# Seven half-block products instead of eight in the last layer's first product, on 512-token blocks

## The chip, the cores and the metric

One core of one Trainium2 chip. The metric is the device time of one execution in microseconds (us). Five engines work side by side, each through its own queue of instructions: TensorE (PE; its weight loads are shown apart, as PEld), VectorE (DVE), ScalarE (ACT), GpSimd (POOL), and SyncE (SP), which issues all the DMAs. Matrix products go to PSUM, eight banks of 128 partitions x 512 floats; everything else lies in SBUF or in DRAM.

## What is computed

Attention with a cumulative bias (4 batches, 8 heads, 576 tokens, 64 per head), then two feed-forward layers, the second with a low-rank mixing of the tokens ahead of it:

```python
def _moe_ref(x, g_ln, w_ch1, w_ch2):            # layer 0; x: (4, 576, 512)
    xn = (x - mu) / np.sqrt(var + 1e-06) * g_ln
    ch = np.maximum(xn @ w_ch1, 0.0) @ w_ch2    # 512 -> 2048 -> 512
    return x + ch

def _moe2_ref(x, U, V, w_ch1, w_ch2):           # layer 1; U: (576, 32), V: (32, 576)
    h = x.transpose(0, 2, 1) @ U @ V
    u = x + h.transpose(0, 2, 1)
    ch = np.maximum(u @ w_ch1, 0.0) @ w_ch2     # 512 -> 2048 -> 512
    return u + ch
```

Weights come as 64-bit floats and are turned into 32-bit ones on the chip.

## The kernel before

**Precision.** Products of the layers run on numbers in two parts: a value is split into hi (fp32r) and lo (the rest), and a product is three matmuls, hi.hi, lo.hi and hi.lo. So each 128 x 128 tile of weights is streamed against by three matmuls, and each of the three has its own weight load.

**Blocks and steps.** The 576 tokens of a batch are block A (256) and block B (320). The hidden 2048 are 16 tiles of 128 (`m`). One step (`st`) is a block and a tile: `mlp1` (lines 1026 to 1066) takes the 4 k-tiles of the 512 inputs, 12 matmuls of 256 or 320 columns (lines 1058 to 1060), into one PSUM bank; ScalarE's relu makes `hh` and a VectorE operation `hl` (lines 1064, 1065). `mlp2` (lines 1068 to 1111) runs `LAG` = 2 steps later: 12 matmuls (lines 1092 to 1094) add the tile's share to the 512 outputs, which stay in PSUM banks (`acc`, and `ps` for block B) until a run of steps of one block ends; then line 1102 adds them to `x`, and in layer 1 line 1106 writes `out`. `GROUPS` (line 31) lists the order of the blocks: layer 0 in six groups, layer 1 as A and B of one batch after the other, each group once with one half of the tiles and once with the other. Attention for later blocks runs between the steps of layer 0.

**Layer 1's input.** `t_items` (line 944) multiplies each finished layer 0 block by U and stores x and that product in DRAM (`x_dr`, `t_dr`). `u_load` and `u_items` (lines 991 to 1020) fetch them, multiply by V (line 1013), add into `x` (line 1017) and split it into `xh` and `xl` (lines 355 to 367), for a block a few steps ahead; `xh` and `xl` have two buffers each, so that the next block's can be made beside the current.

**Weights.** `w_ahead` (line 535) converts and splits a half tile (512 KB in DRAM) during layer 0 and stores it to `w_dr`; `w_split` (line 515) loads the halves from there into 16 SBUF buffers `w`, eight tiles' worth. `mix_prep_v` (line 932) prepares V into two `pB` buffers.

**Order.** Nothing is placed by hand on the engines: each piece is recorded as an operation with a priority (its step), a duration estimate and a choice of engines, and class `Plan` (line 86) lists them in the order in which a greedy walk through the estimates would start them, in five passes. A buffer tag has a fixed number of buffers (`sb` lines 321 to 326), and except for `ps` they are taken in program order. Two operations that go by SBUF alone on VectorE and GpSimd are planned one after the other (`port`).

## Time and profile before

| | us |
|---|---|
| median of 3 runs | 1088.88 (1086.11 to 1090.93) |
| the profiled execution | 1090.13 |
| its span, first to last instruction | 1088.4 |
| TensorE busy in the span | 1066.7 (98%) |
| VectorE busy | 605.4 (56%) |
| ScalarE busy | 497.7 (46%) |
| GpSimd busy | 135.8 (12%) |
| DMA, mean rate | 213.24 MB, 196 GB/s |

A row of a group of instructions reads: line of the kernel, engine, operation, output <- inputs with their shapes, count | busy time, mean ns of one | idle time of the engine ahead of them and what ended it. Matmuls overlap in time and their ends are modelled, so a matmul's own cost is read from the distance between two starts. A DMA row gives the count, the size and the median time from issue to landing.

### The profile page before, as it was taken

The page shows a single profiled execution, that of the slowest core. Times are in us where ns is not written, and L with a number is a line of the kernel's source. Part 1 is how long each engine was busy: PE and PEld are TensorE (multiplying, and loading weights), DVE is VectorE, ACT ScalarE, POOL GpSimd, SP SyncE. Part 2 cuts the span into 40 slices and gives each one's busy share as a digit, 9 for nine tenths or more (in the row PEclk, how much of TensorE's full clock was granted, in tenths as well). Part 3 has the DMA queues.
Part 4 walks back from the last instruction along what each step waited for, and adds up shares of the span by engine and source line. Part 5 has one row for each costly group of instructions (what it writes and reads, how often), then busy time and mean ns, then how long its engine had stood idle before and what let it go on. Part 6 is the DMA issues. An engine that isn't in the chain of part 4 may idle for free.

```text
span 1088.4 us, 20805 instructions
## 1 busy us (share of the span) xinstructions
PE 1066.7 (98%) x7969; PEld 1021.6 (94%) x7969; DVE 605.4 (56%) x1457; ACT 497.7 (46%) x1201; POOL 135.8 (12%) x301
## 2 busy tenths in 40 slices
PE   8998999999999999999999999999999999999998
PEld 6687999999999989988999999999999999999998
DVE  8998976876887766847864535632312331233121
ACT  7988865765765656736654323521211211111110
POOL 1113222231321212301110000000000000000000
PEclk9998999999999999999999999999999999999999
DMA  7998993129735693492368599881154116211710
GB/s 240 352 331 309 357 344 112 60 70 335 250 123 171 223 340 129 149 347 99 131 203 299 190 387 373 296 347 50 49 169 141 49 49 219 91 50 52 258 60 34
DMA packets 76483, 213.24 MB, mean 196 GB/s; under 512 B 11456, under 2 KB 23744, under 8 KB 76384
## 3 DMA queue, kind: packets, MB, share of 16 engines
q1 hardware_dynamic: 76384, 211.91, 55.9%
q8 instruction: 63, 1.03, 0.4%
q14 instruction: 36, 0.29, 0.1%
HBM read 166.71 MB, written 54.60 MB: 203 GB/s over the span
## 4 chain that ended last, share of the span: by engine, by line
PE 84%; DMA 5%; ACT 5%; DVE 4%; issue 1%; POOL 0%; SPq 0%; ACTq 0%; POOLq 0%; DVEq 0%
PE ps L1058 12%; PE ps L1059 11%; PE ps L1060 11%; PE acc L1092 8%; PE acc L1094 8%; PE acc L1093 8%; PE ps L793 4%; PE ps L746 3%; PE ps L1092 3%; PE ps L1093 3%; PE ps L1094 3%; PE ps L697 2%; ACT t L707 1%; PE ps L693 1%; PE ps L675 1%; DMA w<-w_dr 1%
## 5 line engine op out<-in xcount | busy, mean ns | idle before, releaser
L1058 PE MATMUL ps<-xh,w 128*128 128x256 f32 (+1 forms) x1024 | 313.3, 306 | 3.5 <-DVE mx L680 2.6
L1060 PE MATMUL ps<-xl,w 128*128 128x256 f32 (+1 forms) x1024 | 304.0, 297 | 1.0 <-POOL xl L362 1.0
L1059 PE MATMUL ps<-xh,w 128*128 128x256 f32 (+1 forms) x1024 | 303.9, 297 | 0.0
L1065 DVE SCALAR_TENSOR_TENSOR hl<-ps,hh 128x256 fp32r<-128x256 f32 (+1 forms) x256 | 116.5, 456 | 318.2 <-ACT hh L1064 317.1
L1064 ACT ACTIVATE hh<-ps 128x256 fp32r<-128x256 f32 (+1 forms) x256 | 104.2, 408 | 381.6 <-PE ps L1060 380.3
L1092 PE MATMUL acc<-hh,w 128*128 128x256 f32 (+1 forms) x768 | 229.6, 299 | 1.0 <-ACT hh L1064 1.0
L1094 PE MATMUL acc<-hl,w 128*128 128x256 f32 (+1 forms) x768 | 223.9, 292 | 0.5 <-DVE hl L1065 0.5
L1093 PE MATMUL acc<-hh,w 128*128 128x256 f32 (+1 forms) x768 | 223.7, 291 | 0.0
L1058 PEld LDWEIGHTS ps<-xh,w 128*128 128x128 f32 x1024 | 195.4, 191 | 8.5 <-DVE mx L680 2.9
L1060 PEld LDWEIGHTS ps<-xl,w 128*128 128x128 f32 x1024 | 195.0, 190 | 1.3 <-POOL xl L362 1.3
L1059 PEld LDWEIGHTS ps<-xh,w 128*128 128x128 f32 x1024 | 195.6, 191 | 0.5
L1092 PEld LDWEIGHTS acc<-hh,w 128*128 128x128 f32 x768 | 146.0, 190 | 4.3 <-issue 2.0
L1094 PEld LDWEIGHTS acc<-hl,w 128*128 128x128 f32 x768 | 145.9, 190 | 0.8 <-DVE hl L1065 0.7
L1093 PEld LDWEIGHTS acc<-hh,w 128*128 128x128 f32 x768 | 146.1, 190 | 0.5
L707 ACT ACTIVATE t<-t,mx 128x128 f32<-128x128 f32 (+4 forms) x144 | 83.1, 579 | 32.8 <-DVE mx L701 26.5
L1094 PE MATMUL ps<-hl,w 128*128 128x320 f32 x256 | 79.1, 309 | 0.0
L1093 PE MATMUL ps<-hh,w 128*128 128x320 f32 x256 | 79.1, 309 | 0.0
L1092 PE MATMUL ps<-hh,w 128*128 128x320 f32 x256 | 79.1, 309 | 0.0
L360 DVE TENSOR_TENSOR pB<-ps,pB 128x512 fp32r<-128x512 f32 (+2 forms) x114 | 63.4, 570 | 19.2 <-ACT pB L355 18.6
L355 ACT ACTIVATE pB<-ps 128x512 fp32r<-128x512 f32 (+4 forms) x121 | 59.7, 503 | 25.5 <-PE ps L746 23.0
L746 PE MATMUL ps<-ident,t 128*128 128x128 f32 x400 | 64.5, 277 | 6.2 <-POOL t L723 2.0
L701 DVE CUSTOM_DVE_ANT_0 t<-ps,causal 128x128 f32<-128x128 f32 (+3 forms) x128 | 56.9, 487 | 10.6 <-PE ps L697 10.0
(130 smaller groups left out, 1459.7 us busy)
## 6 DMA issues: line engine op xcount, KB each, us to landing
w<-w_dr SPq DMA_DIRECT2D x176, 512.0 KB, 7.1
w_dr<-wr SPq DMA_DIRECT2D x48, 512.0 KB, 4.5
wr<-w1a SPq DMA_DIRECT2D x16, 512.0 KB, 5.9
wr<-w2a SPq DMA_DIRECT2D x16, 512.0 KB, 6.1
w_dr<-w SPq DMA_DIRECT2D x16, 512.0 KB, 6.2
wr<-w1b SPq DMA_DIRECT2D x16, 512.0 KB, 5.0
wr<-w2b SPq DMA_DIRECT2D x16, 512.0 KB, 7.1
qkvB<-qkv_b SPq DMA_DIRECT2D x32, 224.0 KB, 5.4
```

Of the source, the lines that this page charges most:

```text
L355: "act": ((51 if psum else 94) + 0.8333 * n, lambda: nc.scalar.activation(out(), a(), AF.Copy)),
L360: alts = {"dve": (68 + 1.042 * n, lambda: nc.vector.tensor_tensor(out=out(), in0=a(), in1=b(), op=op))}
L707: act(prio, K, lambda t=t, mx=mx, o=o, K=K, x=x, y=nt * z + x: nc.scalar.activation(t[:, o:o + K], t[:, o:o + K], AF.Exp, bias=mx[:, (1 if ...
L746: nc.tensor.transpose(ps[:, 128 * j:128 * (j + 1)], t[:, c:c + 128], ident.tile)
L1058: nc.tensor.matmul(ps[:, :n], w[:, 0, sl], xh[:, k, :n], start=k == 0, stop=False)
L1059: nc.tensor.matmul(ps[:, :n], w[:, 1, sl], xh[:, k, :n], start=False, stop=False)
L1060: nc.tensor.matmul(ps[:, :n], w[:, 0, sl], xl[:, k, :n], start=False, stop=k == KT - 1)
L1064: act(st - 1000, n, lambda: nc.scalar.activation(hh[:, :n], ps[:, :n], AF.Relu), [ps], [hh], 51)
L1065: dve(st - 1000, n, lambda: nc.vector.scalar_tensor_tensor(out=hl[:, :n], in0=ps[:, :n], scalar=0.0, in1=f(hh[:, :n]), op0=ALU.max, op1=AL ...
L1092: nc.tensor.matmul(a, w[:, 0, sl], hh[:, :n], start=new, stop=False)
L1093: nc.tensor.matmul(a, w[:, 1, sl], hh[:, :n], start=False, stop=False)
L1094: nc.tensor.matmul(a, w[:, 0, sl], hl[:, :n], start=False, stop=last and (z == 1 or blk == "B"))
```

## The change

Layer 0 stays as it is. In layer 1:

- The blocks are now C, the first 512 tokens of a batch, and T, the last 64 tokens of all four batches as one block of 256: `LAST = ("C0", "C1", "C2", "C3", "T0")`. Each block goes through all 16 tiles once, in alternating directions.
- **First product of C.** Two tiles (a pair) form a 2 x 2 scheme: two halves of the tokens (256 each), two halves of the 512 inputs (two k-tiles each), two tiles. Eight half-block products give the result directly; here seven do, on sums and differences of operands (Strassen's scheme in Winograd's form). `c_operands` makes the seven operands on the side of the tokens, each split into hi and lo, in the buffers xc, v, xh, xh, xl, xl and t, t: one buffer set for all batches. `w1_ahead` makes the weight sums during layer 0 and stores seven units (hi and lo) per pair; `w1_load` fetches them, 1.84 MB per pair, into two sets of `qk` and `pB` buffers. `mlp1c` runs the products, 6 matmuls of 256 columns each; seven VectorE additions and a copy per pair put the results together in `hh` and `hl` buffers, from which relu and split make the hidden values, in four buffers borrowed from `w`.
- **Second product of C** (`mlp2c`): 12 matmuls per tile as before, each 512 columns wide, into four PSUM banks. Twelve of the 16 tiles of `w2` stay loaded (`W2SLOTS`).
- **T** goes through `mlp1` and `mlp2` as an A block would, on the plain units of the stored weights; x, xh and xl lie in `wr` buffers. Its loads and its `out` DMAs move pieces of 64 tokens (256 bytes).
- V's two parts move from `pB` to `t`; the preparation of layer 1's weights is spread over steps 16 to 132 (`W1`) where it ran over steps 40 to 142, beside other small moves.

```diff
+LAST = ("C0", "C1", "C2", "C3", "T0")
+W2SLOTS = 12
-W1 = (67, 128)
+W1 = (16, 66, 50)
...
+    P.borrow("hw", "w", 2 * WSLOTS - W2SLOTS)
...
+    def w1_ahead(p, gate):
...
+        (ta, tb), s, h = ts, P.buf("wr", [128, 1024]), P.buf("wr", [128, 1024], F32R)
...
+        copy(prio, 256, lambda: s[:, 768:], lambda: tb[:, :256], [tb], [(s, 3)], psum=True)
+        sub(0, lambda: tb[:, 256:], lambda: s[:, 768:], ALU.add, [tb, (s, 3)])
+        sub(2, lambda: ta[:, :256], lambda: s[:, 768:], ALU.subtract, [ta, (s, 3)])
+        sub(1, lambda: s[:, :256], lambda: ta[:, :256], ALU.subtract, [ta, (s, 0)])
+        sub(3, lambda: ta[:, 256:], lambda: s[:, 256:512], ALU.subtract, [ta, (s, 1)])
...
+    OPERANDS = {1: "xc", 5: "v", 6: "xh", 7: "xl", 2: "t", 4: "xh", 3: "xl"}
...
+        known(1, quarter(x0, 0), key(x0, 0))
+        diff(5, quarter(x0, 1), quarter(x0, 0), key(x0, 1), key(x0, 0))
+        diff(6, quarter(x1, 1), sums(5), key(x1, 1), [tmp[5]])
+        known(6, sums(6), [tmp[6]])
+        known(5, sums(5), [tmp[5]])
+        diff(7, quarter(x1, 1), quarter(x0, 1), key(x1, 1), key(x0, 1))
+        known(7, sums(7), [tmp[7]])
+        known(2, quarter(x1, 0), key(x1, 0))
+        diff(4, quarter(x1, 0), sums(6), key(x1, 0), [tmp[6]])
+        known(4, sums(4), [tmp[4]])
+        known(3, quarter(x1, 1), key(x1, 1))
...
+    ORDER = {(0, 0): (1, 6), (0, 1): (7, 5), (1, 0): (2, 4), (1, 1): (3,)}
...
+    def mlp1c(st, half):
...
+                for k in range(2):
+                    sl = slice(128 * k, 128 * (k + 1))
+                    nc.tensor.matmul(region(r), w[:, u, 0, sl], part(r, 0)[:, k], start=new and k == 0, stop=False)
+                    nc.tensor.matmul(region(r), w[:, u, 1, sl], part(r, 0)[:, k], start=False, stop=False)
+                    nc.tensor.matmul(region(r), w[:, u, 0, sl], part(r, 1)[:, k], start=False, stop=k == 1 and (r == 3 or not new))
...
+        if (m % 2, half) == (0, 0):
+            s[1] = P.buf("hh", [128, 256])
+            copy(st - 1000, 256, lambda d=s[1]: d.tile, lambda: region(1), [ps[-1]], [s[1]], psum=True)
+            add(2, "hh", 6, 1)
+        elif half:
+            if m % 2:
+                add(12, "hl", 3, 24)
+                hidden(0, 1, 12)
+            else:
+                add(3, "hh", 7, 2)
+                add(22, "hl", 5, 3)
+                add(24, "hl", 5, 2)
+                hidden(1, 1, 22)
+        else:
+            add(11, "hl", 2, 1)
+            hidden(0, 0, 11)
+            add(21, "hl", 4, 3)
+            hidden(1, 0, 21)
...
+    def mlp2c(st, half):
...
+                nc.tensor.matmul(aa[z].tile, w[:, 0, sl], h[:, 0], start=first, stop=False)
+                nc.tensor.matmul(aa[z].tile, w[:, 1, sl], h[:, 0], start=False, stop=False)
+                nc.tensor.matmul(aa[z].tile, w[:, 0, sl], h[:, 1], start=False, stop=last)
...
+    for n, ((p, tail), users) in enumerate(held):
+        at = NS0 - 14 + 2 * n if n < 2 else held[n - 2][1][-1] + 0.6
+        put(at, lambda q, g, p=p, tail=tail, users=users: w1_load(users[0] - 6, g, p, tail, users))
...
+        elif blk == "C":
+            put(first - 5, lambda p, g, b=b: c_load(p, g, b))
+            for k in range(KT):
+                put(first - 2.75 + 0.25 * k, lambda p, g, b=b, k=k: c_mix(p, b, k))
+            put(first - 1.5, lambda p, g, b=b: c_operands(p, b))
```

## Rows read from the trace of the kernel before

**Rows 1.** The page, parts 1 and 2: busy times and 40 slices.
```profile
PE 1066.7 (98%) x7969; PEld 1021.6 (94%) x7969; DVE 605.4 (56%) x1457; ACT 497.7 (46%) x1201; POOL 135.8 (12%) x301
...
DVE  8998976876887766847864535632312331233121
ACT  7988865765765656736654323521211211111110
...
PEclk9998999999999999999999999999999999999999
```

**Rows 2.** Stages: stretch, length, busy time and count per engine, PEclk, DMA share, GB/s.
```profile
110.00:661.00 551.00, 542.75 (x4045) 517.20 (x4046) 378.90 (x923) 321.52 (x754) 108.51 (x243) 1.00 0.63 218
661.00:680.00 19.00, 19.00 (x149) 18.70 (x148) 10.75 (x22) 7.04 (x16) 0.88 (x1) 1.00 0.95 362
680.00:760.00 80.00, 80.00 (x597) 79.64 (x597) 33.30 (x59) 24.11 (x50) 0.00 (x0) 1.00 0.65 236
760.00:1088.00 328.00, 325.02 (x2431) 324.75 (x2429) 84.67 (x186) 51.81 (x125) 2.71 (x3) 1.00 0.30 101
```

**Rows 3.** The same table over two stretches of layer 0.
```profile
100.00:200.00 100.00, 96.69 (x818) 91.45 (x817) 76.86 (x218) 69.00 (x192) 23.27 (x50) 1.00 0.71 248
200.00:300.00 100.00, 98.92 (x802) 95.00 (x802) 77.16 (x191) 67.67 (x159) 28.48 (x66) 1.00 0.57 194
```

**Rows 4.** Timeline of TensorE in layer 1: start, duration (us), engine, line, operation.
```profile
899.73 0.31 PE L1058 MATMUL ps<-xh,w 128*128 128x320 f32 x1
...
900.61 0.28 PE L1092 MATMUL acc<-hh,w 128*128 128x256 f32 x1
900.73 0.28 PE L1093 MATMUL acc<-hh,w 128*128 128x256 f32 x1
...
902.04 0.31 PE L1058 MATMUL ps<-xh,w 128*128 128x320 f32 x1
```

**Rows 5.** TensorE's groups of instructions after 661 us, shapes apart.
```profile
L1060 PE MATMUL ps<-xl,w 128*128 128x320 f32 x258 | 79.7, 309 | 0.0
...
L1092 PE MATMUL acc<-hh,w 128*128 128x256 f32 x256 | 72.6, 283 | 0.0
...
L1092 PE MATMUL acc<-hh,w 128*128 128x320 f32 x132 | 40.9, 310 | 0.0
```

**Rows 6.** Timeline of TensorE around two pairs of 512-wide matmuls.
```profile
672.43 0.39 PE L968 MATMUL ps<-xs,u 128*128 128x512 f32 x1
672.66 0.40 PE L969 MATMUL ps<-xs,u 128*128 128x512 f32 x1
672.89 0.28 PE L1058 MATMUL ps<-xh,w 128*128 128x256 f32 x1
...
336.85 0.39 PE L968 MATMUL ps<-xs,u 128*128 128x512 f32 x1
337.08 0.40 PE L969 MATMUL ps<-xs,u 128*128 128x512 f32 x1
337.31 0.28 PE L1058 MATMUL ps<-xh,w 128*128 128x256 f32 x1
```

**Rows 7.** Timeline of TensorE: transposes of 128 columns in a stream.
```profile
205.06 1.69 PE L746 MATMUL ps<-ident,t 128*128 128x128 f32 x14
206.50 0.36 PE L1092 MATMUL acc<-hh,w 128*128 128x256 f32 x1
```

**Rows 8.** Groups of VectorE and ScalarE by shape: what a 256 and a 512 operation take.
```profile
L1065 DVE SCALAR_TENSOR_TENSOR hl<-ps,hh 128x256 fp32r<-128x256 f32 x128 | 53.9, 422 | 140.9 <-ACT hh L1064 140.4
L360 DVE TENSOR_TENSOR wr<-ps,wr 128x512 fp32r<-128x512 f32 x48 | 33.0, 687 | 10.6 <-ACT wr L355 10.1
L1102 DVE TENSOR_TENSOR x<-x,acc 128x512 f32<-128x512 f32 x32 | 21.9, 686 | 11.6 <-PE acc L1094 11.4
L360 DVE TENSOR_TENSOR xl<-xc,xh 128x256 fp32r<-128x256 f32 x11 | 5.3, 529 | 0.0
L360 DVE TENSOR_TENSOR xl<-x,xh 128x256 fp32r<-128x256 f32 x12 | 5.1, 422 | 0.4
L355 ACT ACTIVATE qk<-qk 128x512 fp32r<-128x512 f32 x5 | 3.1, 627 | 1.8 <-DMA qk<-qkvA 1.8
```

**Rows 9.** Conversions of weights after 661 us: groups of ScalarE and VectorE.
```profile
L488 ACT ACTIVATE wr<-wr 128x512 int32<-128x512 uint32 x9 | 6.0, 670 | 0.0
L490 DVE SCALAR_TENSOR_TENSOR ps<-ps,wr 128x512 uint32<-128x512 uint32 x9 | 6.3, 698 | 1.8 <-ACT wr L488 1.6
```

**Rows 10.** DMA issues: count, KB each, median us to landing.
```profile
out<-x SPq DMA_DIRECT2D x16, 128.0 KB, 1.8
...
wr<-U SPq DMA_DIRECT2D x1, 128.0 KB, 5.9
```

More of the change, by code (lines that the diff above doesn't have):

```diff
@@ L172, in slot @@
                 lst = live[tag]
-                over = len(lst) + n - self.cap[tag]
+                over = len(lst) + n - cap[tag]
                 if over > 0:
+                    base, most = self.take.get(tag, (None, 0))
+                    if cap[tag] < most:
+                        assert cap[tag] + n <= most and base not in need
+                        lst = live[base]
                     done = sorted(gone(b, e) for b in lst if not b.users)
@@ L446, in mha_ffn_mixer_ffn @@
                     runs.append(run)
+    NS0 = len(steps)
+    for n, x in enumerate(LAST):
+        run = {"blk": (1, int(x[1]), x[0])}
+        for p in range(HALF):
+            for z in range(2):
+                steps.append((*run["blk"], 2 * (HALF - 1 - p if n % 2 else p) + z))
+                runs.append(run)
     NS = len(steps)
@@ new lines, in t_load, with t_mix, mm @@
+    def t_load(prio, gate):
+        x = xt[0, "T"] = P.buf("wr", [128, KT, 256])
+        for b in range(B):
+            load(prio, 128 * 1024, lambda b=b: nc.sync.dma_start(x[:, :, 64 * b:64 * (b + 1)], x_dr[b, "B"][:, :, 256:]), [x_dr[b, "B"]], [(x, b)], gate, 150.0)
+    def t_mix(prio, gate, b):
+        x, t, ps = xt[0, "T"], mixed(prio, gate, b), psum()
+        def mm():
+            for k in range(KT):
+                for z, vv in enumerate(v4):
+                    nc.tensor.matmul(ps[:, 64 * k:64 * (k + 1)], t[:, 128 * k:128 * (k + 1)], vv[:, 512:], start=z == 0 and k == 0, stop=z == 1 and k == KT - 1)
+        pe(prio - 500, 8 * 109, mm, [t] + v4, [ps])
+        dve(prio, 256, lambda: nc.vector.tensor_tensor(
+            out=x[:, :, 64 * b:64 * (b + 1)], in0=x[:, :, 64 * b:64 * (b + 1)], in1=ps[:, :256].rearrange("p (k c) -> p k c", c=64), op=ALU.add),
+            [ps, (x, b)], [(x, b)])
@@ new lines, in mlp2c, with mm @@
+    def mlp2c(st, half):
+        _, b, _, m = steps[st]
+        w, h = w2t[st], hbuf[st]
+        ks = (0, 1) if half == 0 else (2, 3)
+        run = runs[st]
+        first, last = st == run["first"], st == run["last"]
+        if first:
+            run[half] = [P.buf("acc", [128, 512]), psum()]
+        aa = run[half]
+        def mm():
+            for z, k in enumerate(ks):
+                sl = slice(128 * k, 128 * (k + 1))
+                nc.tensor.matmul(aa[z].tile, w[:, 0, sl], h[:, 0], start=first, stop=False)
+                nc.tensor.matmul(aa[z].tile, w[:, 1, sl], h[:, 0], start=False, stop=False)
+                nc.tensor.matmul(aa[z].tile, w[:, 0, sl], h[:, 1], start=False, stop=last)
+        free2[st] = pe(st + LAG + 0.5, 6 * mm_cost(512), mm, [w, h], aa)
+        if last:
+            x = xt[b, "C"][0][half]
+            for z, a in enumerate(aa):
+                kk = [(x, (z, y)) for y in range(2)]
+                k = ks[z]
+                dve(st - 1000, 512, lambda a=a, z=z: nc.vector.tensor_tensor(out=x[:, z], in0=x[:, z], in1=a.tile, op=ALU.add), [a] + kk, kk)
+                load(st - 1000, 128 * 2048, lambda k=k, z=z: nc.sync.dma_start(out[128 * k:128 * (k + 1), b * S:b * S + 512], x[:, z]), kk, [])
+            if half == 1:
+                xt.pop((b, "C"))
+        if half == 1:
+            del hbuf[st]
@@ L1069, in mlp2 @@
         l, b, blk, m = steps[st]
[L1070 to L1071 removed]
+        if blk == "C":
+            mlp2c(st, half)
+            return
+        n = BLK[blk][1]
+        w = w2t[st] if l else inst[step_w[st]]["w", 1]
         _, hh, hl = hbuf[st]
@@ new lines, in w2_load @@
+    def w2_load(prio, gate, m, users):
+        w = P.buf("w", [128, 2, 512], F32R)
+        load(prio, 128 * 4096, lambda: nc.sync.dma_start(f(w.tile), w2_dr[m].tile), [w2_dr[m]], [w], gate)
+        for st in users:
+            w2t[st] = w
+    held, loads = [], []
+    for st in range(NS0, NS, 2):
+        _, _, blk, m = steps[st]
+        old = next((x for x in held[-2:] if x[0] == (m // 2, blk == "T")), None)
+        if old is None:
+            old = [(m // 2, blk == "T"), []]
+            held.append(old)
+        old[1] += [st, st + 1]
@@ new lines, in mha_ffn_mixer_ffn @@
+    for n, ((p, tail), users) in enumerate(held):
+        at = NS0 - 14 + 2 * n if n < 2 else held[n - 2][1][-1] + 0.6
+        put(at, lambda q, g, p=p, tail=tail, users=users: w1_load(users[0] - 6, g, p, tail, users))
+    held = []
+    for st in range(NS0, NS):
+        m = steps[st][3]
+        last = {}
+        for x in held:
+            last[x[0]] = x
+        live = sorted(last.values(), key=lambda x: x[1][-1])[-W2SLOTS:]
+        old = next((x for x in live if x[0] == m), None)
+        if old is None:
+            old = [m, [], live[0][1][-1] if len(live) == W2SLOTS else None]
+            held.append(old)
+        old[1].append(st)
@@ L1143, in mha_ffn_mixer_ffn @@
+    for n, (m, users, after) in enumerate(held):
+        at = inst[len(inst) - WSLOTS + n // 2]["last"] + LAG + 1 + 0.5 * (n % 2) if after is None else after + LAG + 0.8
+        put(at, lambda p, g, m=m, users=users, after=after: w2_load(users[0] - 6, g if after is None else free2[after], m, users))
     put(12, lambda p, g: mix_prep_u(p))
```

291 lines of the change are left out of this document (194 added, 97 removed).

## The prediction

> **What bounds the kernel now.** First the page's shares and slices [rows 1]: TensorE is busy 98% of the span and its clock reads 9 tenths or more in every slice, while VectorE and ScalarE fall to 1 to 3 tenths in the last third. Next the stages [rows 2]: layer 1 begins near 661 us; from there on TensorE has no idle stretch and VectorE works 129 of 427 us. In 110 to 661 us TensorE is idle 8.3 us of 551, with VectorE at 69% and ScalarE at 58%. The groups of layer 1 [rows 5] say the same: no idle time stands before any of them. So layer 1 lasts as long as its matmuls take to stream. What one costs is not the mean that the groups give (283 or 309 ns, ends overlap) but the distance between starts. [Rows 4]: six 320-wide ones take 899.73 to 900.61 us, 0.1467 us each; twelve 256-wide ones 900.61 to 902.04 us, 0.1192 us each. The counts of [rows 5] times these give the stage: about 1560 wide ones (28 of them layer 0's rest) and 1536 narrow ones, with the mixing products, come to 423 us, and the stage runs from 661 to 1085 us. Nothing else has to be explained.
>
> **Before, the part that is replaced.** Each of layer 1's two products has 4 batches x 16 tiles x 4 x 3 = 768 matmuls of 256 and 768 of 320 columns. Both products: 1536 x 0.1467 + 1536 x 0.1192 = 225.3 + 183.1 = 408.4 us. Mixing (line 1013) is 32 of each: 8.5 us. Together 416.9 us.
>
> **After, the same part.** (a) First product: per batch 8 pairs of tiles x 7 products x 2 x 3 = 336 matmuls, 1344 in all, 256 wide: 160.2 us. Eight products would be 1536, so the seventh saved is 22.9 us; against that the 64 tokens that stood inside the 320 now go apart. (b) Second product: 768 matmuls of 512 columns. The trace has only single pairs of that width [rows 6]: 672.43, 672.66, 672.89 and 336.85, 337.08, 337.31, so 0.23 each; over eight clean pairs the mean is 0.231. The ends: 0.2285 if the step from 256 to 320 columns (27.5 ns for 64) goes on, rounded down a little, and 0.2385 if a 512 costs two 256s. I take 0.231, because it is the row of this very width: 177.4 us (175.5 to 183.2). (c) The 4 x 64 last tokens as one 256-wide block: 192 + 192 matmuls, 45.8 us. (d) Mixing: 32 of 512 columns, 7.4 us, and 32 of 64 columns. No row shows 64 columns in a stream; the nearest are transposes of 128, 14 of them in 205.06 to 206.50 us, 0.103 each [rows 7]: 3.3 us (between 0 and 3.8, the last at 0.1192). Sum 394.1 us. **TensorE saves 22.8 us** (17 to 28, the upper end with free 64-column mixing).
>
> A rule speaks about term (b). The Trainium skill, TensorE: Matmul & The Clock Gate, section Back-to-back issue gap, gives an isolated gap of N/2.4 + 2.5 ns, so some 216 ns for 512 columns; the rows above have 230 for it, and 119 where the rule gives 109. By the rule term (b) would be about 166 us and the saving 34 us; the measurement decides here. What the mechanism would be without the page: the 13 ns that rows 4 show above 256/2.4 and 320/2.4 come from the weight load before every matmul and vanish where the matmul is longer. That is 768 x 0.013 = 10 us more, and 768 x (0.231 - 0.2133) = 13.6 us if a 512 streams in 512/2.4 exactly. This is rival 1.
>
> **What is added elsewhere, and what covers it.** *Layer 0.* The weight sums: per pair a copy, four 256-wide VectorE operations of about 0.42 us and two splits of 512 (ScalarE 0.627, VectorE 0.687 each) [rows 8]; for 8 pairs about 24 us VectorE and 13 us ScalarE. And the conversions still done after 661 us, nine half tiles [rows 9] of about 2.07 us VectorE and 1.9 us ScalarE, must be done before layer 1: 19 and 17 us. VectorE in 110 to 661 goes from 379 to 422 us, 77%; ScalarE to 352, 64%. TensorE's 8.3 us of work cover this almost wholly; without cover it is 43 us. The stretch that is at 77% now loses somewhat more than the later ones, and the planner's order changes everywhere, so I add 1.5 us (-3, as the order may also come out better, to +10). More DMA too: about 8 MB more written, at a share of 0.63 [rows 2].
>
> *Entry into the first block.* The sums s2 and s3 sit in the three hh buffers, hh and hl free in order, so they wait for layer 0's last two second products (12 x 0.1467 each). The block's first steps run 24 x 0.1192 + 1.76 + 18 x 0.1192 + 1.76 = 8.5 us before the last is free; then five additions of 0.42, ScalarE's relu and a subtraction, some 3.5 us with their waits, against the 2.9 us until the first wide product wants them. +1 us (0 to 4).
>
> *Block boundaries.* The seven operands fill every buffer of xc, v, xh and xl, and t too, so the next batch's are written only as the last pair's products release them, one by one. A pair lasts 42 x 0.1192 + 24 x 0.231 = 10.55 us, and each operand has about that long until its product comes round. VectorE then has 11 SBUF subtractions of 0.687 (7.6 us), four drains and four mixing additions (5.5 us), beside 11 operations of 0.42 per pair (4.6 us): some 23 us in two pairs of 21, over three pairs 28 of 32; ScalarE takes the seven copies. It fits when the order is good. +1 us for three boundaries (0 to 25). *Weights.* 26 loads of 1.84 MB, each with some 13 us between the release of its buffers and its first use, and 32 of 0.52 MB: in the last block (5.7 us per pair, 1.05 MB, 7 us of room) +0.5 us (0 to 5).
>
> *Tail.* Now two 686 ns additions instead of pairs of 490, then pieces of 256 B instead of 1,280. [Rows 10]: out of 128 KB lands in 1.8 us; the nearest to the new form is U's 128 KB in 256 B pieces, 5.9 us, read in a crowded stretch. +1 us (0 to 4.1).
>
> **Sum.** The profiled execution took 1090.1 us, 1.2 above the median. 1090.1 - 22.8 + 1.5 + 1 + 1 + 0.5 + 1 = 1072.3; less 1.2 gives **1071 us**.
>
> **The rivals.** *1. Wide matmuls cheaper*: 1071 - 10 to 13.6, some 1059 us. For: the fixed 13 ns of rows 4. Against: rows 6. *2. Layer 0 lengthens*: a quarter of the 43 us on VectorE shows, as waits before transposes and products: +10, 1081 us. For: VectorE at 77% throughout. Against: the stretch from 100 to 300 us stands at 77% already and loses 4.4 of 200 us [rows 3], 2.2%; that share of 551 us would be 12 us, 4 more than now. *3. Boundaries wait*: an operand's copy or subtraction stands at the head of an engine's queue before its buffer is released, and the sums of the last pair stand behind it; the result banks are not drained, and TensorE stops. Price about 4 us at each of three boundaries and the entry: +16, 1087 us. It decides once the operands need over the 10.55 us of a pair. For: single buffers, and 23 us of VectorE in 21. A rule for it: the Trainium skill, GPSIMD Engine Reference, section Specifications, has GpSimd contend with VectorE instructions with two SBUF inputs, so GpSimd could not relieve these subtractions for nothing. The rows agree: xl from xc and xh at 256 took 529 ns in layer 0, from x and xh 422 in layer 1, where GpSimd is idle [rows 8]. *4. Weights arrive late in the first block (slower)*: it loads 8 x 1.84 + 16 x 0.52 MB, with the stores of the last layer 0 block and the next block's x about 25 MB, in 84 us, 300 GB/s. For: 680 to 760 us moved 236 GB/s and the span 196. Against: 661 to 680 us moved 362 [rows 2], and 236 may have been all that was asked. At 236 the block takes 107 us, +23: 1094 us; at 196, 128 us: 1115 us. Slower by 0.5% from about 236 GB/s down.
>
> **How the numbers follow.** Forecast 0.54 (1064 to 1079), rival 1 0.09, rival 2 0.15, rival 3 0.12, rival 4 0.10. A measurement of this kernel can tell some 0.5%, 5.4 us, from no change: faster means under 1083.4. Faster: 0.54 + 0.09 + 0.15 and a sixth of rival 3, 0.80; within: the rest of rival 3, 0.10; slower: rival 4, 0.10. The range from 1057 to 1084 holds the forecast, rivals 1 and 2 and that sixth: 0.80.
>
> **What would show it.** Start to start 0.231 us in the wide product and 0.119 in the seven; layer 1 from its first product to the last about 400 us instead of 424; TensorE idle in 110 to 661 us under 12 us; waits of the new first product on operand buffers of at most 1 or 2 us at the three boundaries; no wait of it on a weight load. The forecast is wrong if 512 columns cost 0.216 or over 0.24, or if TensorE's idle time in layer 1 is over 10 us.

## The result, and the profile after

| | before | after |
|---|---|---|
| median, us | 1087.49 (1085.59 to 1090.93, 4 runs) | **1071.3** (1070.44 to 1072.25, 4 runs) |
| the profiled execution, us | 1090.13 | 1071.02 |
| its span, us | 1088.4 | 1069.2 |

After over before is 0.9848, with an interval from 0.9819 to 0.9877. The forecast was 1071. The total fits better than its terms do: two of them are off by some 5 us in opposite directions, as the traces show. One execution of the experiment e7 further down took 1665.7 us at a mean granted clock of 0.56 and is left out of its median and ratio.

The page of the kernel after, as [rows 1] before: busy time, then the slices of TensorE, VectorE, GpSimd and the granted clock.

```profile
PE 1042.1 (97%) x7393; PEld 960.0 (90%) x7393; DVE 709.3 (66%) x1744; ACT 508.5 (48%) x1224; POOL 175.5 (16%) x333
...
PE   9998999999999999989999999999999999999998
...
DVE  7999978886798766685785533755645744744521
...
POOL 1123213241341232211420000200100200200000
PEclk9998999999999999999999999999999999999999
```

TensorE still bounds the kernel. VectorE, which before stood at 1 to 3 tenths in the last third, now stands at 4 to 7 there: the sums of the seven products. By stage, as [rows 2] (busy time of each engine, then granted clock, DMA share and GB/s):

```profile
110.00:661.00 551.00, 538.99 (x4002) 510.14 (x4001) 393.95 (x957) 330.73 (x776) 127.43 (x261) 1.00 0.71 243
661.00:680.00 19.00, 19.00 (x143) 18.64 (x142) 17.53 (x38) 10.39 (x22) 5.49 (x4) 1.00 0.97 357
680.00:760.00 80.00, 80.00 (x498) 71.37 (x496) 49.57 (x118) 21.13 (x45) 5.91 (x4) 1.00 0.72 256
760.00:1069.00 309.00, 303.09 (x2003) 277.78 (x2001) 149.19 (x363) 52.42 (x123) 12.44 (x9) 1.00 0.56 189
```

In 110 to 661 us TensorE is idle 12.0 us instead of 8.3. The page's list of waits for 661 us to the end holds one line for TensorE, at the first product of T:

```profile
PE ps L1277 <- DMA pB<-w_dr: 0.9, 1, 0.9
```

So nothing waited at the entry into layer 1 or at the three boundaries. The cadence, as [rows 4] and [rows 6], from the order of TensorE's instructions at the first boundary (start, duration, line):

```profile
742.57 0.28 PE L1199 MATMUL ps<-xc,pB 128*128 128x256 f32 x1
...
751.35 0.40 PE L1236 MATMUL acc<-w,w 128*128 128x512 f32 x1
...
754.09 0.28 PE L1199 MATMUL ps<-xl,qk 128*128 128x256 f32 x1
...
754.80 0.28 PE L1199 MATMUL ps<-xc,pB 128*128 128x256 f32 x1
...
756.92 0.40 PE L1236 MATMUL acc<-w,w 128*128 128x512 f32 x1
...
759.67 0.28 PE L1199 MATMUL ps<-t,pB 128*128 128x256 f32 x1
...
761.75 0.40 PE L1236 MATMUL acc<-w,w 128*128 128x512 f32 x1
```

The first batch's last pair starts at 742.57, the second batch's first pair at 754.80. Twelve 512-wide ones take 751.35 to 754.09, 0.228 us each; then come one product of the scheme (6 matmuls, 0.71 us) and the next batch. The operands of the second batch are made meanwhile, from the first split of xc to the last subtraction for xh (ScalarE and VectorE):

```profile
745.46 0.63 ACT L374 ACTIVATE xc<-x 128x512 fp32r<-128x512 f32 x1
755.24 0.68 DVE L379 TENSOR_TENSOR xh<-xs,xh 128x512 fp32r<-128x512 f32 x1
```

Second products that the first batch still owes stand between the first products of the second (756.92, 761.75). The engines around this boundary:

```profile
743.00:764.00 21.00, 21.00 (x130) 18.84 (x129) 15.92 (x36) 6.75 (x14) 4.54 (x3) 1.00 0.17 47
```

Over all such stretches of layer 1, start to start: before, 1536 matmuls of 256 at 0.1202 (184.6 us), 1536 of 320 at 0.1467 (225.3 us) and mixing 8.5, together 418.4 us. After: 1344 in the first product at 0.1173 (157.7), 768 of 512 at 0.2297 (176.4), T 45.8, mixing 7.4 and 3.2, together 390.5 us. **Streaming fell by 27.9 us, the span by 19.1** (1088.35 to 1069.24). The missing 8.8 us:

- the wait of T, 0.9;
- the tail, 1.9: the span ends 5.57 us after the start of the last matmul (1063.67), before 3.64 us (1084.71);
- by difference, 6.0 ahead of layer 1's stream. Of these 3.8 are idle time of TensorE in 110 to 661 us; in 0 to 110 us it is idle 1.1 less; the other 3.3 lie in stretches that count as busy, where starts stand further apart than the median of their shape (0.8 more than before in 0 to 110 us, 1.5 in 110 to 300, 1.0 in 500 to 661).

This compares one execution with one. The profiled execution of the kernel before is 2.6 us above its median; by the medians the kernels are 16.2 us apart, and some 9 us would stand where 6.0 stands.

The last outputs, VectorE's additions and SP's stores of the kernel after, then the stores of the kernel before (for a row of SP: time of the first issue, time of all the issues):

```profile
1063.27 1.40 DVE L1320 TENSOR_TENSOR wr<-wr,acc 128x512 f32<-128x512 f32 x2 [2.04 <-PE acc L1312]
1063.99 2.71 SPq L1324 DMA_DIRECT2D out<-wr  x4
```

```profile
1084.25 1.80 SPq L1106 DMA_DIRECT2D out<-x  x4
```

The stores start 0.3 us after the last matmul's start, before 0.5 us ahead of it: two additions of 0.69 drain the sums where there were four of 0.49, and the first ends later. Issuing the four takes 2.71 us instead of 1.80, so the last goes out another 0.7 us later, and it lands 2.4 us after its issue instead of 1.9. Together these are the 1.9 us; the end of the span follows 0.8 us after the landing in both. The second addition ends at 1064.68, while SP is still issuing the second store (1064.65 to 1065.29), so no store waits for it.

### The profile page after: what moved, and what is told of

It is laid out like the page before. It is cut to its first block, busy times and chain, and to the rows that moved or that the text cites. A ratio compares the mean times of both kernels' runs of the same rounds, so it can differ in the third digit from the quotient of the medians.

```text
span 1069.2 us, 20135 instructions
## 1 busy us (share of the span) xinstructions
PE 1042.1 (97%) x7393; PEld 960.0 (90%) x7393; DVE 709.3 (66%) x1744; ACT 508.5 (48%) x1224; POOL 175.5 (16%) x333
## 4 chain that ended last, share of the span: by engine, by line
PE 70%; DMA 11%; DVE 8%; ACT 6%; issue 2%; SPq 1%; POOL 1%; DVEq 0%; ACTq 0%; POOLq 0%
PE ps L1199 5%; PE ps L1201 5%; PE ps L1200 5%; PE ps L1277 5%; PE ps L1279 4%; PE ps L1278 4%; PE acc L1310 3%; PE acc L1312 3%; PE acc L1311 3%; PE acc L1236 3%; PE acc L1237 3%; PE ps L1236 3%; PE ps L1237 3%; PE acc L1238 3%; PE ps L1238 3%; PE ps L853 3%
## 5 line engine op out<-in xcount | busy, mean ns | idle before, releaser
L1277 PE MATMUL ps<-xh,w 128*128 128x256 f32 (+1 forms) x512 | 160.5, 314 | 3.3 <-DVE mx L761 1.9
L1279 PE MATMUL ps<-xl,w 128*128 128x256 f32 (+1 forms) x512 | 152.5, 298 | 1.2 <-POOL xl L381 1.2
L1278 PE MATMUL ps<-xh,w 128*128 128x256 f32 (+1 forms) x512 | 152.4, 298 | 0.0
L1310 PE MATMUL acc<-hh,w 128*128 128x256 f32 (+1 forms) x448 | 136.6, 305 | 0.5 <-ACT hh L1283 0.5
L1312 PE MATMUL acc<-hl,w 128*128 128x256 f32 (+1 forms) x448 | 130.1, 290 | 0.6 <-DVE hl L1284 0.6
L1311 PE MATMUL acc<-hh,w 128*128 128x256 f32 (+1 forms) x448 | 129.9, 290 | 0.0
L1277 PEld LDWEIGHTS ps<-xh,w 128*128 128x128 f32 x512 | 98.1, 192 | 9.3 <-issue 2.7
L1279 PEld LDWEIGHTS ps<-xl,w 128*128 128x128 f32 x512 | 97.8, 191 | 1.5 <-POOL xl L381 1.5
L1278 PEld LDWEIGHTS ps<-xh,w 128*128 128x128 f32 x512 | 98.2, 192 | 0.7
L1310 PEld LDWEIGHTS acc<-hh,w 128*128 128x128 f32 x448 | 85.2, 190 | 3.4 <-issue 1.8
L1312 PEld LDWEIGHTS acc<-hl,w 128*128 128x128 f32 x448 | 85.1, 190 | 1.1 <-DVE hl L1284 1.1
L1311 PEld LDWEIGHTS acc<-hh,w 128*128 128x128 f32 x448 | 85.3, 191 | 0.3
L379 DVE TENSOR_TENSOR pB<-ps,pB 128x512 fp32r<-128x512 f32 (+1 forms) x112 | 62.6, 571 | 14.3 <-ACT pB L374 13.6
L374 ACT ACTIVATE pB<-ps 128x384 fp32r<-128x384 f32 (+3 forms) x115 | 56.5, 500 | 18.7 <-PE ps L806 18.0
```

What stands on the lines that cost most here:

```text
L1277: nc.tensor.matmul(ps[:, :n], lhs(k, 0), xh[:, k, :n], start=k == 0, stop=False)
L1278: nc.tensor.matmul(ps[:, :n], lhs(k, 1), xh[:, k, :n], start=False, stop=False)
L1279: nc.tensor.matmul(ps[:, :n], lhs(k, 0), xl[:, k, :n], start=False, stop=k == KT - 1)
L1310: nc.tensor.matmul(a, w[:, 0, sl], hh[:, :n], start=new, stop=False)
L1311: nc.tensor.matmul(a, w[:, 1, sl], hh[:, :n], start=False, stop=False)
L1312: nc.tensor.matmul(a, w[:, 0, sl], hl[:, :n], start=False, stop=last and (z == 1 or blk == "B"))
```

## The experiments

Where the first product of C starts splits each execution in two: what lies ahead is layer 0 (with the weights' preparation), what lies behind is layer 1. For the kernel after this is the first start in the row of the line that streams operand xc (min, median and max of a duration, first and last start):

```profile
L1199 PE MATMUL ps<-xc,pB x64: 276/281/376, 668.1 to 998.8; 128*128 128x256 f32 x64
```

and 1069.24 - 668.06 = 401.2 us are left to the end. For all kernels (us; medians beside the kernel before in the same session, ratio with its interval):

| kernel | median | ratio to before | layer 1 starts | from there to the end |
|---|---|---|---|---|
| after | 1071.3 | 0.9848 [0.9819, 0.9877] | 668.1 | 401.2 |
| e5 plain product, 512 wide | 1095.4 | 1.0070 [1.0044, 1.0096] | 670.3 | 423.1 |
| e1 the same, T's loads shared | 1100.1 | 1.0120 [1.0092, 1.0148] | 669.5 | 430.1 |
| e2 second product 256 wide | 1081.6 | 0.9943 [0.9923, 0.9962] | 668.8 | 412.0 |
| e3 no weight sums | 1069.6 | 0.9842 [0.9816, 0.9869] | 664.2 | 402.8 |
| e7 weight sums twice | 1089.1 | 0.9994 [0.9972, 1.0016] | 685.5 | 404.1 |
| e6 operands split twice | 1082.1 | 0.9946 [0.9924, 0.9968] | 670.1 | 408.1 |
| e8 weights prepared later | 1086.4 | 0.9982 [0.9963, 1.0001] | 679.4 | 407.4 |
| e10 weights prepared earlier | 1101.4 | 1.0128 [1.0103, 1.0154] | 696.9 | 402.4 |
| e4 T's result stored plainly | 1072.5 | 0.9872 [0.9829, 0.9916] | 672.3 | 401.9 |
| e9 T ahead of the last C block | 1071.6 | 0.9852 [0.9830, 0.9874] | 670.1 | 401.1 |
| e11 another order | 1079.0 | 0.9917 [0.9887, 0.9947] | 669.9 | 401.7 |
| e12 before, another order | 1090.0 | 1.0020 [0.9995, 1.0045] | | |

One thing must be known to read the fourth column. In e1, e2, e4, e5, e6 and e9 the planner gave layer 0 the order that it has in the kernel after: TensorE, VectorE, ScalarE and GpSimd run the same sequence of operations up to at least 629 us, in e4 to the end of the kernel. The start of layer 1 in these six and in the kernel after, 668.1 to 672.3 us, is therefore what one execution of the same work differs from another, and the kernel after is the earliest of the seven. e3, e7, e8, e10 and e11 have other orders.

### Where the gain comes from: e1, e5 and e2

e1 keeps the blocks C and T and takes the seven products back: per tile four k-tiles, three matmuls of 512 each, with relu and subtraction straight from the bank.

```diff
-        for r in ORDER[m % 2, half]:
-            tag, u = UNIT[r]
...
-                for k in range(2):
-                    nc.tensor.matmul(region(r), w[:, u, 0, sl], part(r, 0)[:, k], start=new and k == 0, stop=False)
...
+            for k in ks:
+                xh, xl = hi[k // 2][:, k % 2], lo[k // 2][:, k % 2]
+                nc.tensor.matmul(ps.tile, lhs(k, 0), xh, start=k == 0, stop=False)
+                nc.tensor.matmul(ps.tile, lhs(k, 1), xh, start=False, stop=False)
+                nc.tensor.matmul(ps.tile, lhs(k, 0), xl, start=False, stop=k == KT - 1)
```

> Undoes the seven products alone: the first product of the 512-token blocks goes by 12 plain matmuls of 512 columns per tile, on unsummed operands and weights; layer 0 with its weight sums, the wide second product and the block of last tokens stay. Theory (layer 1 lasts as long as its matmuls stream): 768 x 0.229 = 175.9 us instead of 1344 x 0.118 = 158.6, so +17 us, about 1088 us, and no new waits of TensorE in layer 1. Rival (the seven products bring nothing of their own, the wide blocks bring it all): 1071 to 1075 us.

Measured: 1100.06, more than either theory gave. Part of it was made by the edit: it let T share its weight loads with the last block, and T waited. The wait, and the stretches around it (busy time, granted clock):

```profile
PE ps L1203 <- DMA pB<-w_dr: 5.1, 1, 5.1
```

```profile
1040.00:1050.00 10.00, 10.00 (x76) 9.57 (x75) 3.81 (x7) 1.15 (x3) 0.00 (x0) 1.00 0.71 221
1050.00:1066.00 16.00, 10.89 (x69) 10.68 (x68) 1.27 (x3) 1.15 (x3) 0.00 (x0) 0.79 0.63 241
1066.00:1085.00 19.00, 19.00 (x162) 19.00 (x161) 2.55 (x6) 2.30 (x6) 0.00 (x0) 1.00 0.53 179
```

The granted clock of the stretch with the wait is 0.79, and the wait costs more than itself: the 27 matmuls of 256 behind it start 0.213 us apart or more instead of 0.119, 2.7 us more. Layer 1 is 7.0 us longer than in e5, below, of which the longer wait is 4.2 us. e5 gives T its own loads, as in the kernel after:

```diff
-        tags = {"pB": (4, 8)} if tail else {"qk": (0, 3), "pB": (3, 7)}
+        tags = {"pB": (4, 8)}
...
-        old = next((x for x in held[-2:] if x[0] == (m // 2, True)), None)
+        old = next((x for x in held[-2:] if x[0] == (m // 2, blk == "T")), None)
```

> The first run with plain 512-wide first products again, with one thing mended: the last block loads its weight units by itself, as the changed kernel does, instead of sharing the loads of the block before it (there TensorE waited 5.1 us for them and its clock fell behind the wait). Theory: 768 first products at the 0.233 us of that run, 179 us, instead of 158, so +21 us, 1092 us, with a wait of at most 1 to 2 us before the last block. Rival (the seven products bring little; the 29 us of the first run were its wait and what followed): 1075 to 1080 us.

Measured: 1095.43; T's wait is 0.9 us, as in the kernel after. The row of its first product:

```profile
L1139 PE MATMUL ps<-xh,pB x128: 392/394/504, 670.3 to 941.0; 128*128 128x512 f32 x128
```

Layer 0 has the same order and ends 2.2 us later than in the kernel after (670.3 against 668.1), and from there it is 423.1 us against 401.2: **the seven products are worth 21.9 us**, where the prediction had 22.9. By cadence: 768 of 512 at 0.2335 are 179.3 us, 1344 of 256 at 0.1173 are 157.7, a difference of 21.6. The median is 24.1 us above that of the kernel after, 3 us more than expected. The rival of e5, that the gain lies in the wide blocks, falls: with the wide blocks and the plain product the kernel is 0.7% slower than before (interval 0.44% to 0.96%). This kernel still makes the weight sums that it has no use for. Its streaming is 179.3 + 176.4 + 45.8 + 10.6 = 412.1 us, 6.3 less than before: of the 27.9 us of streaming the seven products bring 21.6 and the widths 6.3, which is less than what the change adds elsewhere.

e2 goes the other way and runs the second product as two halves of 256, with the seven products kept:

```diff
-                nc.tensor.matmul(aa[z].tile, w[:, 0, sl], h[:, 0], start=first, stop=False)
-                nc.tensor.matmul(aa[z].tile, w[:, 1, sl], h[:, 0], start=False, stop=False)
-                nc.tensor.matmul(aa[z].tile, w[:, 0, sl], h[:, 1], start=False, stop=last)
+                for c in range(2):
+                    cs = slice(256 * c, 256 * (c + 1))
+                    nc.tensor.matmul(aa[z][:, cs], w[:, 0, sl], h[:, 0, cs], start=first and c == 0, stop=False)
+                    nc.tensor.matmul(aa[z][:, cs], w[:, 1, sl], h[:, 0, cs], start=False, stop=False)
+                    nc.tensor.matmul(aa[z][:, cs], w[:, 0, sl], h[:, 1, cs], start=False, stop=last and c == 1)
```

> Undoes the width of the second product alone: 24 matmuls of 256 columns per tile instead of 12 of 512, the seven products stay. Theory: 1536 x 0.119 = 182.8 us instead of 768 x 0.229 = 175.9, +7 us, about 1078 us. Rival (a 512 costs as much as two 256, and the width brought nothing): 1071 us.

Measured: 1081.63. 1536 of 256 at 0.1200 are 184.3 us, 7.9 more than 768 of 512; with 2.3 us more of waits in layer 1 than after (3.1 against 0.9, 1.7 of them at T) that is 10.2 of the 10.9 us of the table. The theory's 7 us is the streaming; it had no waits. The rival, that width doesn't matter, falls; a wide matmul is cheaper by 10 ns than two of 256 (0.2297 against 2 x 0.1200), and the forecast's 0.231 is off by 1.3 ns.

### What the weight sums cost: e3 and e7

```diff
-        copy(prio, 256, lambda: s[:, 768:], lambda: tb[:, :256], [tb], [(s, 3)], psum=True)
-        sub(0, lambda: tb[:, 256:], lambda: s[:, 768:], ALU.add, [tb, (s, 3)])
...
-            split(prio, 512, lambda sl=sl: h[:, sl], lambda sl=sl: s[:, sl].bitcast(F32R), lambda sl=sl: s[:, sl], kk, [(h, q)], kk)
-        for z, a in enumerate((h, s)):
+        for z, a in enumerate(raws):
```

> Leaves out the weight sums of layer 0 (the copy, four additions and two splits per pair); raw units are stored in their place, with the same DMAs, so the output is that of other weights in layer 1. Theory (the 12.0 us that TensorE is idle in 110 to 661 us, where the kernel before had 8.3, come from the elementwise work added there): idle 8 to 9.5 us, about 1068 us. Rival (the added idle time is the new order of everything, not that work): idle 11 to 13 us, 1070 to 1072 us.

Measured: 1069.56. Layer 0:

```profile
110.00:661.00 551.00, 542.18 (x4024) 513.59 (x4024) 383.26 (x930) 329.12 (x771) 111.28 (x248) 1.00 0.72 246
```

TensorE is idle 8.8 us (after: 12.0; before: 8.3), as the theory had it, and layer 1 starts at 664.2, 3.8 us before the earliest of the seven executions with the sums. VectorE does 10.7 us less and GpSimd 16.1 us less: by busy time, more than half of what goes had been on GpSimd. The order is another one too, from 170 us on. In layer 1, where the same matmuls run, 1.6 us come back (a wait of 0.5 for `x` and 0.2 more at T among them; the rest was not traced), so the median falls by less than 2 us.

e7 does the copy, the four sums and the two splits twice over (`for _ in range(2):` around them); the stores stay single.

> The weight sums of layer 0 (copy, four additions, two splits per pair) are done twice. Theory (layer 0 got longer because of this work: TensorE idle 12.0 us in 110 to 661 us with it, 8.8 us without it): idle 14 to 16 us, 1073 to 1076 us. Rival (the order, not the amount): 11 to 13 us, 1070 to 1072 us.

Measured: 1089.05, some 13 us beyond the expectation. Layer 0, and what TensorE waited for in it (us, times, longest):

```profile
110.00:661.00 551.00, 527.15 (x3884) 497.61 (x3885) 416.74 (x1026) 333.98 (x779) 117.68 (x247) 0.99 0.69 232
```

```profile
PE ps L807 <- POOL t L711: 3.2, 1, 3.2
PE ps L1278 <- DVE pB L379: 2.7, 3, 2.1
PE ps L1278 <- DMA w<-w_dr: 2.6, 2, 2.0
PE acc L1311 <- DMA w<-w_dr: 2.4, 1, 2.4
```

Idle is 23.9 us, and layer 1 starts at 685.5, 17.4 later. VectorE is here at 416.7 us, near the 422 that the prediction had for the kernel after. The waits on `w` are not for VectorE but for loads from `w_dr`, 5.0 us in the two rows; whether those were late because the weights ahead of them were converted and stored later was not traced. The sums done once cost 3.8 us against e3, done twice 17.4 more, and loads are late that the sums don't touch; so the work did not simply fill idle time up to a limit. But e7 is another order as well, and such a change alone moved the median by 7.7 us (e11, below): how much of the 17.4 us the sums make is not shown.

### Entry and boundaries: e6 and e8

```diff
         def known(r, src, reads):
-            split(prio, 512, lambda: part(r, 0), lambda: part(r, 1), src, reads, [(op[r][0], 0)], [(op[r][1], 1)])
+            for _ in range(2):
+                split(prio, 512, lambda: part(r, 0), lambda: part(r, 1), src, reads, [(op[r][0], 0)], [(op[r][1], 1)])
```

> Every split of the seven operands into its two parts is done twice, 7 x (0.627 us ScalarE + 0.687 us VectorE) more per batch. Theory (the boundaries cost nothing because second products are still to be run while the operands are made): no or little wait of TensorE at the three boundaries, 0 to 3 us more in all, 1071 to 1074 us. Rival 3 of the prediction in its weaker form (the operands just fit into a pair's time): 4.8 us per boundary show, 1083 to 1086 us.

Measured: 1082.1, near the rival by its size, but not at its place. TensorE's waits of layer 1, the longest:

```profile
PE ps L1202 <- DVE xl L379: 1.2, 1, 1.2
PE ps L1278 <- DMA pB<-w_dr: 1.2, 2, 1.0
PE ps L1200 <- ACT xl L374: 1.0, 1, 1.0
PE ps L1202 <- DVE xh L379: 0.8, 2, 0.6
```

Those for operands lie between 673.93 and 684.28 us, in the first block, 3.7 us together; none for an operand lies at the three boundaries, where there was twice the work too (VectorE is busy 18.5 to 19.4 of the 21 us around each). So the boundaries had room for double their splits, and the entry had not. In the table layer 1 is 6.9 us longer; 5.1 of it are waits beyond T's 0.9. Layer 1 starts 2.0 later, which is within the spread of that order, and the rest of the 10.8 us between the medians was not traced.

e8 moves the preparation of layer 1's weights some six steps later, e10 as far forward:

```diff
-W1 = (16, 66, 50)
+W1 = (22, 70, 44)
```

> One size changed: the preparation of layer 1's weights is placed later and closer to its use (W1 = (22, 70, 44), so that the first half runs over steps 22 to 92 and the last tile is at 130 instead of 126). Theory: VectorE is freer in the later part of layer 0 (66 to 69% at 400 to 600 us against 79 to 84% at 100 to 400 us in the changed kernel), so TensorE's idle time in 110 to 661 us falls to 9 to 11 us, 1068 to 1071 us. Rival (late weights are then waited for in the first block of layer 1): waits there of 2 us and more, 1072 to 1076 us.

Measured: 1086.37; both expectations missed. TensorE's idle time in 110 to 661 us is 13.6 us, where 9 to 11 were expected. Layer 1 starts 11.4 us later, 3.2 of it by the first wait here, and its first operands are late:

```profile
PE ps L1199 <- ACT xc L374: 3.2, 1, 3.2
PE acc L1236 <- ACT xs L374: 1.5, 1, 1.5
PE ps L1201 <- POOL xc L381: 1.0, 1, 1.0
```

The entry is the place of e6's waits too: here, later weights are converted when the operands of the first block are to be made, on ScalarE directly before the first split:

```profile
677.73 0.58 ACT L374 ACTIVATE wr<-ps 128x512 fp32r<-128x512 f32 x1
678.21 0.66 ACT L511 ACTIVATE wr<-wr 128x512 int32<-128x512 uint32 x1
678.77 0.62 ACT L374 ACTIVATE xc<-x 128x512 fp32r<-128x512 f32 x1
```

The rest of the 11.4 us was not located. e10 is the move forward:

```diff
-W1 = (16, 66, 50)
+W1 = (10, 62, 56)
```

> The changed kernel with layer 1's weight preparation begun earlier and ended earlier (W1 = 10, 62, 56 instead of 16, 66, 50; moving it later, by 6 steps, gave 1086). If the preparation's place sets the waits, by what it collides with, then earlier frees the entry into layer 1 but loads the first half of layer 0, where VectorE is busiest: TensorE idle in 110 to 661 us 13 to 20 instead of 12, no wait behind 661: 1072 to 1080. Rival: any other place draws a different order of everything, and 1071 is the best of the orders that were around: 1080 or more, with waits in several stretches.

Measured: 1101.39, the slowest of all, 28.8 us of it ahead of layer 1. The longest wait and the stretches around it, then what stood ahead of it on VectorE and SP (for the row of three: time of the first issue, time of all):

```profile
PE ps L1277 <- DMA w<-w_dr: 8.1, 1, 8.1
```

```profile
150.00:160.00 10.00, 6.66 (x48) 5.42 (x47) 6.91 (x22) 8.06 (x23) 1.42 (x4) 0.84 0.92 298
160.00:170.00 10.00, 2.82 (x12) 2.53 (x12) 6.65 (x13) 3.75 (x8) 0.73 (x1) 0.50 0.87 287
```

```profile
160.07 0.69 DVE L379 TENSOR_TENSOR wr<-ps,wr 128x512 fp32r<-128x512 f32 x1
160.78 3.99 SPq L561 DMA_DIRECT2D w_dr<-wr  x3
165.79 0.32 SPq L545 DMA_DIRECT2D w<-w_dr  x1
170.92 0.55 PE L1277 MATMUL ps<-xh,w 128*128 128x256 f32 x1 [8.09 <-DMA w<-w_dr]
```

Layer 0's own weights come late here, by a chain: VectorE ends a split of them at 160.76, the store goes out at 160.78 and lands at 165.77, the load goes out at 165.79 and lands at 170.78. Each transfer took 5.0 us, less than the 7.5 us that is the median of such loads in this run. So it was not the transfer that was slow, though the DMA engines are nearly full (0.92 and 0.87): the split came late, and why it did was not traced. In the slice that TensorE spends mostly idle the granted clock is 0.50, its lower level of 1.2 GHz. By its number the rival holds (1080 or more, waits in several stretches): TensorE is idle 13.8 us in 100 to 200, and 5.2 and 5.3 us in 400 to 500 and 500 to 600. The theory had 13 to 20 us of idle time in 110 to 661; it is 28.1. Layer 1 itself is about as long as after (402.4 us).

### The tail: e4 and e9

e4 stores T's result as whole rows to a scratch tensor; the last 64 tokens of each batch stay unwritten.

```diff
-                    load(st - 1000, 512 * n, lambda k=k: nc.sync.dma_start(
-                        out[128 * k:128 * (k + 1)].rearrange("p (b s) -> p b s", b=B)[:, :, 512:], x[:, k].rearrange("p (b c) -> p b c", b=B)), kk, [], None, 150.0)
+                    load(st - 1000, 512 * n, lambda k=k: nc.sync.dma_start(o_dr[k].tile, x[:, k]), kk, [o_dr[k]], None, 350.0)
```

> The last block writes its result as whole rows of 256 tokens to a scratch tensor instead of pieces of 64 tokens into the output, so the last 64 tokens of each batch are left unwritten. Theory (the 256-byte pieces lengthen the tail: 5.4 us from the last matmul to the end of the span against 3.4 before): the tail falls to about 4 us, 1069.5 to 1070 us. Rival (the tail is the drain of two 512-wide sums and the fixed time of a DMA): tail 5 to 5.5 us, 1071 us.

Measured: from the last matmul (1068.99 us) to the end of the span 5.2 us, against 5.57: the rival's range. SP's issues take 0.32 to 0.44 us instead of 0.60 to 0.66, and the last goes out 0.7 us sooner, but it lands 2.7 us later instead of 2.4: the pieces of 256 B cost 0.3 us of the tail. The median (1072.53) says nothing on it: the four executions took 1068.8 to 1077.2 us, and in the profiled one (1076.1) layer 1 starts at 672.3, 4.2 us later than in the kernel after. TensorE, VectorE, ScalarE and GpSimd run the same operations in the same order in both kernels, and SP's issues differ only in the last four stores. So the same order of the same work moves by some 8 us from one execution to another; what moves it was not traced.

```diff
-LAST = ("C0", "C1", "C2", "C3", "T0")
+LAST = ("C0", "C1", "C2", "T0", "C3")
```

> The changed kernel with T one place earlier, between the third and the fourth C block (LAST = C0, C1, C2, T0, C3); nothing else. The last block is then a C block, whose two products keep more work queued. My theory: T's wait of 0.9 us on a weight load is covered or stays, T's switch costs nothing else, and the tail is set by the last block's drains: four additions of 512 wide into x and four stores of 256 KB instead of two additions and four small-piece stores, so 0 to 2 us longer: 1070 to 1074. Rival: the last 64 tokens at the end cost more than the 5.5 us of tail that they show, because a block with half the matmuls per loaded weight outruns its loads: then 1066 to 1069.

Measured: 1071.63, in the theory's range and no different from the kernel after, but not as the theory had it. The tail is 4.3 us (1066.86 to 1071.2) instead of 5.6, shorter where it should have been up to 2 us longer; T's wait is 1.6 instead of 0.9. Layer 1 is as long in both (401.1 and 401.2 us).

### The order alone: e11 and e12

Both change one number of the planner's prices, e11 in the kernel after, e12 in the kernel before. The work is the same; order and some choices of engines are others.

```diff
-                price[e][w] = max(0.0, price[e][w] + 0.75 * (use[e][w] - mean))
+                price[e][w] = max(0.0, price[e][w] + 0.8 * (use[e][w] - mean))
```

> The changed kernel with one number of the planner's prices changed (the weight of a window's load when an engine is chosen, 0.8 instead of 0.75): the same work, another order of it and some operations on another engine. It measures how far the order alone moves the time. Theory: order alone moves layer 0 by a few us: 1068 to 1076, with layer 1's stretch within 2 us of 400. Rival: the order alone is worth 10 us or more either way, so that the differences of 10 to 18 us found when operands, sums or weights were changed can't be put down to their work.

> The kernel before with the one number of the planner's prices changed to 0.8 that was changed in the kernel after for e11: the same work as before in another order. The changed kernel went from 1071 to 1079 by it. Theory: both kernels' orders are draws from a spread of some 10 us, almost all of it in layer 0, and the gain of layer 1 stands apart from it: before in the other order between 1085 and 1100, so that the changed kernel in the same other order is faster than it by 10 to 25 us. Rival: the kernel after is faster because its order happens to be good: then before in the other order is at 1080 or less, about as fast as e11.

Measured: e11 1078.99 (1074.09 to 1081.84), between the two expectations, with layer 1 as the theory had it (401.7 us); e12 1089.98 (1084.52 to 1095.78), in the theory's range, and its rival falls. Layer 0 of e11, then of e12:

```profile
110.00:661.00 551.00, 538.57 (x3990) 510.24 (x3991) 400.48 (x968) 330.98 (x775) 123.71 (x256) 1.00 0.71 242
```

```profile
110.00:661.00 551.00, 541.65 (x4025) 516.23 (x4024) 375.57 (x913) 318.34 (x753) 118.57 (x256) 0.99 0.63 218
```

The profiled execution of e11 was its shortest, and it shows 1.8 us more ahead of layer 1 and 0.5 behind; where its others lose up to 8 us more was not seen. In the other order the changed kernel is still faster, by 11 us, so the gain is not a draw of the order alone. About 5 of the 16 us may be: the difference of 5 is about as wide as the intervals of the ratios that it is taken from. The executions of the kernel after lie within 2 us of each other, but those of e4, in the same order, 8 us apart.

## Why the prediction was right, step by step

| step | predicted, us | shown, us |
|---|---|---|
| TensorE's streaming | -22.8 (17 to 28) | -27.9 |
| layer 0 | +1.5 (-3 to +10) | +6.0, by difference (some 9 by the medians) |
| entry | +1 | 0 |
| three boundaries | +1 | 0 |
| weights, T | +0.5 | +0.9 |
| tail | +1 | +1.9 |
| sum, on the span | -17.8 | -19.1 |

**What bounds it** was read rightly: layer 1 lasts as long as its matmuls stream, after as before, and the seventh saved product is worth 21.9 us (e5 against after) where 22.9 stood. Of the signs that the prediction named, one stands at its limit: TensorE's idle time in 110 to 661 us, 12.0 us where under 12 was called for.

**The size of the saving** was too small by 5.1 us, for want of rows. Six and twelve matmuls were the sample of [rows 4]. Over the whole stage the 256-wide ones before cost 0.1202 and not 0.1192 (1.5 us), the new ones 0.1173 and not 0.1192 (2.5 us), the 512-wide ones 0.2297 and not 0.231 (1.0 us); each by 1 to 2 ns, and with 768 to 1536 of them that is microseconds. The price of a 512 was the disputed term: rival 1 needed 0.2133 to 0.218, the traces show 0.2297, so it falls. The isolated gap of the Trainium skill (TensorE: Matmul & The Clock Gate, Back-to-back issue gap), 216 ns for 512 columns and 109 for 256, is not met in this stream at either width (230, and 117 to 120).

**Layer 0** was the weak term: 6.0 us instead of 1.5, inside the bounds, and nearer to rival 2's 10 us than to the forecast; rival 2 misses the total only because the streaming saved more. The work that the step listed is there, but it went elsewhere: VectorE rose by 15 us instead of 43, GpSimd by 19, ScalarE by 9 instead of 30; and five half tiles more, not nine, were converted before 661 us (60 rows against 55; four remain, in place of the nine of [rows 9]). The step had given GpSimd nothing. At about the VectorE time that it foresaw, 416.7 us, e7 has 23.9 us of idle time, 15.6 more than before: there rival 2 would have been the better forecast (though e7 is another order too). So it was not the cover of 77% that held, as the step has it; less work came on VectorE than it said. How much of the 6.0 us is the sums' is open: without them layer 1 starts 3.8 us earlier (e3), but executions of one and the same order of layer 0 differ in that start by up to 4.2 us (668.1 to 672.3).

**Entry and boundaries**: no wait at either, and rival 3 falls for the boundaries: twice the splits there make no wait (e6). Its sum, 23 us of VectorE in two pairs of 21, was too large: around the three boundaries VectorE is busy 15.9, 15.5 and 15.3 of 21 us, and GpSimd, to which the sum gave nothing, 4.5 to 5.6 us with the subtractions that it took over. The entry is another matter: more work there shows as waits (3.7 us for operands in e6, 4.2 for xc in e8).

**Weights** of the first block: rival 4 falls. In 680 to 760 us the kernel moved 256 GB/s, in 661 to 680 us 357, and no first product of C waited for a load; 236 GB/s was what was asked for, and no limit. In the last block 0.9 us, where 0.5 stood.

**Tail**: +1.9 where +1 stood. The bound from U's pieces, 5.9 us, was far off: the stores land in 2.4 to 2.8 us, and the small pieces matter by 0.3 us (e4). Its parts are a later first store (0.8), longer issues (0.7) and a later landing (0.5); the prediction listed the additions and the landing, not the issues.

So the forecast's closeness is luck in part: the two wrong sizes, 5.1 us of saving and 4.5 us or more of layer 0, stand against each other. What is no luck is the bound by streaming and the price of the seventh product.

## What to carry over

Where one engine streams without a pause, a product fewer is worth what its matmuls cost from start to start, here 22 of 22.9 us; take that distance over hundreds of matmuls, since 1 ns on 3000 of them is 3 us. The same order of the same work took 1068.8 to 1077.2 us in four executions (e4), and another order of it moved the median by 7.7 us (e11) and by 2 us (e12), so measure both before a difference of that size is put down to an edit; and compare the sequences of operations of two traces before saying that the order changed. Added preparation can cost more than the idle time of its engine suggests: look for what is queued behind it, late weight loads among them.
